# Attention and top-1 experts on one core: transposes de-interleaved on the PSUM read, masks from two iotas, unordered scatters, gathers without fills, paired score tiles

## The chip, the core and the metric

The kernel runs on one core of a Trainium2 chip. The time is the device time of one launch in microseconds (us), as the median of several runs. Beside it stands one profiled execution, from which all rows here come.

## What is computed

Attention over 4 batches of 8 heads, 768 positions of 64 numbers; heads 0, 2 and 6 see all earlier positions, the other five see four sink positions and a window of 64. Its output, seen as 3072 rows of 512, goes through an early-exit layer: a row whose skip score is positive goes to the one expert (of eight, 512 to 1024 to 512) with the highest gate logit.

```python
causal = rel >= 0                                  # rel = row - column
stream_keep = causal & (is_sink | ((rel >= 0) & (rel < window)))
mask = np.where(retr[0, :, 0, 0, None, None], causal, stream_keep)
scores = np.where(mask[None], 0.125 * (q @ k.transpose(0, 1, 3, 2)), -1e9)
a = np.exp(scores - scores.max(-1, keepdims=True))
x = (a / (a.sum(-1, keepdims=True) + 1e-09)) @ v   # to rows of 512
do_compute = x @ w_skip > 0
xc = x[do_compute]
logits = xc @ w_gate
e_idx, gate_w = argmax, and softmax at it
y[mask] = gate_w[mask, None] * (np.maximum(xc[mask] @ w1[e], 0.0) @ w2[e])   # mask = e_idx == e
out = x.copy(); out[do_compute] = xc + y
```

With the fixed draw 1163 rows are computed, by expert 69, 235, 250, 230, 53, 142, 42 and 142.

## The kernel before

The attention runs in turns `b` = 0 to 4 (the loop over `range(B + 1)` at the end of the attention part). In turn b the scores of batch b are made and, woven into them, the outputs of batch b - 1. A turn begins with `prep_v(b)` on POOL: the ones column of `va` (L249), copies of it into `vs` shifted by half a row tile (L253, L254), and zeros (L255). Then, for each of six row tiles i, comes `avx(b-1, i)` and a sixth of the steps of `front(b)`; after them `route(b-1)`, and the loads for later turns: q and k of b + 2, V of b + 2 (six DMAs, L108), and the weights of expert b + 1. All these loads convert to f16 on the way and are issued by POOL. q, k and V have two buffers each, the weights five.

`front(b)` handles four head pairs. `trans` transposes a pair's q and k on PE, six row tiles each, into a PSUM tile `tps` (64 + 64 features by six tiles by 128 rows), which is evicted to `qT` or `kT`. The rows lie in memory so that row p of tile n is position 6p + n, so the eviction writes with a stride of six elements (12 bytes); it is done in turn by DVE (L271) and ACT (L269):

```python
o = t.rearrange("c (p n) -> c n p", n=NT)
if ev[0] % 2: nc.scalar.copy(o, ps)
else:         nc.vector.tensor_copy(o, ps)
```

`retr` makes the scores of a retrieval head in three column chunks (L296, exp L301 on ACT, the triangle on DVE L307), `strm` those of a streaming head (L316 and L320, exp L323, mask `smask` on DVE L324), `sinks` those against the sink positions. `avx(b, i)` multiplies them with V (L343 to L359), normalises on DVE (L362, L363), sends the rows `x` to the output by DMA, casts them to f16 on POOL (L368, `x16`), transposes them on PE (L371, again into a `tps`), copies them to `xT` on ACT (L374) and multiplies by the gate weights (L377, `lps`, copied to `lg` on DVE, L380). The two PSUM buffers with tag "t" are shared by all transposes, gate logits and routing products; the scores have two others.

`route(b)` finds for each row its expert and its rank there (`oh`, L398; `rps`, L402 to L407), and adds its row number and gate, in three f16 parts, to the table `tab` by products with one-hot matrices (L452, L454). The table has 16 slots (two tiles of 128 for each of eight experts) by 128.

After the attention, `emp`, `idf` and `idx` (L512 to L516) turn the table into row numbers, an empty slot's being one beyond the bounds check. `gather(e)` fills `xg` with zeros on DVE (L529) and fetches its rows from the output in memory with an indirect DMA (L530), which skips empty slots. `up_(e)` casts (L550), transposes (L553), multiplies by w1 (L562) and applies ReLU; `down(e)` multiplies by w2 (L577), adds gate times result to `xg` (L579), and scatters the rows back with an indirect DMA (L581). All scatters write the same output tensor, so each waits for the one before. A branch for experts with over 256 rows (L604, L605) isn't taken here.

Which instruction stands where on its engine is set by the scheduler of the Tile framework, from the order of the code and the buffers. The DMAs of POOL's queue use eight semaphores (DMASW0 to DMASW7) in turn: one may be issued when the DMA eight before it, which had its semaphore, has landed.

Of the kernel before, what the change touches and what calls it, by code (L numbers as in the profile page):

```python
# [9 lines left out]
FP32 = mybir.dt.float32  # L10
# [41 lines left out]
def kernel(  # L52
# [59 lines left out]
    def load_w(e):  # L112
# [5 lines left out]

    load_qk(0, True)
# [12 lines left out]
    nc.vector.memset(utri, 1.0)  # L132
    nc.gpsimd.affine_select(out=utri, in_=utri, compare_op=ALU.is_ge, fill=0.0,
                            base=-1, pattern=[[1, P]], channel_multiplier=-1)
# [7 lines left out]
    nc.vector.memset(smask, 1.0)  # L142
    nc.gpsimd.affine_select(
        out=smask[:D], in_=smask[:D], compare_op=ALU.is_ge, fill=0.0,
        base=0, pattern=[[0, NT], [1, P]], channel_multiplier=-1)
    nc.gpsimd.affine_select(
        out=smask[:D], in_=smask[:D], compare_op=ALU.is_ge, fill=0.0,
        base=WINDOW - 1, pattern=[[0, NT], [-1, P]], channel_multiplier=1)

    nc.gpsimd.memset(smask[:N_SINK, 0, N_SINK:], 1.0)  # L150

    up = smask.rearrange("p i c -> p (i c)")
    nc.gpsimd.memset(up[D:, :D], 0.0)
    mid = up[D:, D:D + 5 * P].rearrange("p (i c) -> p i c", c=P)
    nc.gpsimd.affine_select(
        out=mid, in_=mid, compare_op=ALU.is_ge, fill=0.0,
        base=0, pattern=[[0, 5], [1, P]], channel_multiplier=-1)
    nc.gpsimd.affine_select(
        out=mid, in_=mid, compare_op=ALU.is_ge, fill=0.0,
        base=WINDOW - 1, pattern=[[0, 5], [-1, P]], channel_multiplier=1)  # L160
    last = up[D:, D + 5 * P:]
    nc.gpsimd.affine_select(
        out=last, in_=last, compare_op=ALU.is_ge, fill=0.0,
        base=0, pattern=[[1, D]], channel_multiplier=-1)
# [92 lines left out]
    def trans(b, pr):  # L257
        for name, src, dst in (("qT", q_in[b], qT), ("kT", k_in[b], kT)):
# [207 lines left out]
    def front(b):  # L466

        yield lambda: trans(b, 0)
        for c in range(3):
            yield lambda c=c: retr(b, 0, (0, 1), c)  # L470
            if c == 0:
                yield lambda: trans(b, 1)
# [234 lines left out]
```

## Time and profile before

| | |
|---|---|
| median of 3 runs | 318.55 us (318.13 to 319.8) |
| profiled execution | 318.38 us, span 316.6 us |
| busy PE, PE weight loads | 209.7 us, 133.7 us |
| busy DVE, ACT, POOL | 153.5, 124.7, 126.2 us |
| moved by the DMA queues | 37.7 MB, 119 GB/s on average |
| end of the last matmul | 280.15 us |

PE is TensorE, DVE is VectorE, ACT ScalarE, POOL GpSimd. A busy share over the whole span says little here, as the parts of the program have different limits; the rows below are therefore taken by stretches. In a row, "[3.86 <-DMA va]" says that the engine stood idle for 3.86 us before this instruction and that a DMA into va released it. "a<-b" names output and inputs of a group.

### The profile page before, as it was taken

To read this page: it belongs to the slowest core of one execution; us is meant where nothing else is said; L and a number is where in the kernel's file an instruction comes from. 1 tells how busy PE (TensorE), PEld (TensorE's weight loads), DVE (VectorE), ACT (ScalarE), POOL (GpSimd) and SP (SyncE) were. 2 spreads that over 40 slices of the span, in tenths; PEclk is the share of its full clock that TensorE was granted. 3 is DMA by queue.
4 is the path that set the end of the run, shared out by engine and by line. 5 is a ranking of instruction groups with operands and counts; after the bars stand their busy time and mean duration, and the time that the engine had idled before them with its cause. 6 is when DMAs were issued, how large, how long until landed. Compare 5 with 4: busy or idle time off the path is not lost. (4 is left out here: it accounts for less than half of the span.)

```text
span 316.6 us, 5049 instructions
## 1 busy us (share of the span) xinstructions
PE 209.7 (66%) x1996; PEld 133.7 (42%) x1996; DVE 153.5 (48%) x406; ACT 124.7 (39%) x137; POOL 126.2 (40%) x190
## 2 busy tenths in 40 slices
PE   0148589798755999668998897116999999930000
PEld 0133346446534546444455564104766666610000
DVE  2169354635855256896455765743444444320000
ACT  1149930869604578606676521102322222200000
POOL 8998597153328107341011112037853121222321
PEclk9999999999999999999999999999999999985555
DMA  6999999999999997911001022005499969120110
GB/s 90 158 53 143 169 206 247 224 207 223 221 183 219 236 187 103 68 35 66 35 0 68 14 88 75 28 18 153 100 188 204 219 123 167 57 81 20 41 40 6
DMA packets 53457, 37.71 MB, mean 119 GB/s; under 512 B 28706, under 2 KB 45090, under 8 KB 53424
## 3 DMA queue, kind: packets, MB, share of 16 engines
q0 software_dynamic: 49968, 31.01, 67.5%
q10 hardware_dynamic: 1728, 3.15, 2.9%
q1 hardware_dynamic: 1728, 3.15, 2.8%
q8 instruction: 17, 0.28, 0.4%
q14 instruction: 16, 0.13, 0.1%
HBM read 56.66 MB, written 10.49 MB: 212 GB/s over the span
## 5 line engine op out<-in xcount | busy, mean ns | idle before, releaser
L269 ACT COPY kT<-tps 128x768 f16<-128x768 f16 x16 | 43.5, 2716 | 26.5 <-PE tps L262 26.5
L271 DVE COPY qT<-tps 128x768 f16<-128x768 f16 x16 | 43.5, 2720 | 17.5 <-PE tps L262 17.1
L301 ACT ACTIVATE atr<-sps 128x1024 f16<-128x1024 f32 (+1 forms) x36 | 32.9, 948 | 17.7 <-PE sps L296 17.6
L581 POOL DMA_INDIRECT out_dram<-xg,idx x16 | 15.9, 997 | 56.8 <-DMA out_dram<-xg,idx 34.4
L368 POOL CAST x<-x 128x512 f16<-128x512 f32 x24 | 15.0, 627 | 43.0 <-DVE x L363 23.5
L562 PE MATMUL mhp<-mxT,w1t 128*128 128x256 f16 x256 | 30.8, 281 | 1.1 <-ACT mxT L555 0.4
L577 PE MATMUL myp<-w2t,ht 128*128 128x512 f16 x128 | 29.9, 379 | 0.0
L296 PE MATMUL sps<-qT,kT 64*128 64x512 f16 (+3 forms) x96 | 28.3, 474 | 2.0 <-ACT kT L269 2.0
L374 ACT COPY xT<-tps 128x512 f16<-128x512 f16 x24 | 14.1, 588 | 39.0 <-PE tps L371 19.4
L562 PEld LDWEIGHTS <-w1t 128*128 128x128 f16 x256 | 25.8, 101 | 7.3 <-issue 2.8
L371 PE MATMUL tps<-ident,x 128*128 128x128 f16 x96 | 15.2, 302 | 19.1 <-DVE qT L271 12.3
L352 PE MATMUL av<-va,atr 128*128 128x65 f16 x252 | 24.9, 243 | 0.0
L108 POOL DMA_DIRECT2D va<-in_v_dram x24 | 21.2, 933 | 7.5 <-DMA w1t<-in_moe_w_dram 4.9
L262 PE MATMUL tps<-ident,qin 128*64 128x128 f16 x192 | 13.7, 312 | 15.6 <-POOL ident masks.py:199 13.4
L530 POOL DMA_INDIRECT xg<-out_dram,idx x16 | 16.5, 1029 | 17.4 <-DVE idx L516 12.8
L555 ACT COPY mxT<-mtp 128x512 f16<-128x512 f16 x16 | 8.7, 588 | 35.5 <-PE mtp L553 35.5
L566 DVE TENSOR_SCALAR ht<-mhp 128x512 f16<-128x512 f32 x16 | 11.1, 692 | 23.7 <-PE mhp L562 23.7
L362 DVE RECIPROCAL rec<-av 128x4 f32<-128x4 f32 x48 | 8.5, 182 | 28.2 <-PE av L352 20.9
L343 PE MATMUL av<-vsk,esk 20*128 20x260 f16 x48 | 18.8, 394 | 2.9 <-DVE x L363 1.7
L363 DVE TENSOR_TENSOR x<-av,rec 128x256 f32<-128x256 f32 x48 | 19.9, 420 | 1.6
L352 PEld LDWEIGHTS <-atr 128*128 128x128 f16 x252 | 15.9, 123 | 9.5 <-issue 7.6
L357 PE MATMUL av<-vs,ats 128*64 128x65 f16 x120 | 19.4, 254 | 0.7 <-DVE ats L324 0.7
(131 smaller groups left out, 388.0 us busy)
## 6 DMA issues: line engine op xcount, KB each, us to landing
w1t<-in_moe_w_dram POOLq DMA_DIRECT2D x8, 1024.0 KB, 14.2
w2t<-in_moe_w_dram POOLq DMA_DIRECT2D x8, 1024.0 KB, 15.9
va<-in_v_dram POOLq DMA_DIRECT2D x24, 128.0 KB, 10.1
out_dram<-x ACTq DMA_DIRECT2D x12, 256.0 KB, 4.9
out_dram<-x SPq DMA_DIRECT2D x12, 256.0 KB, 2.8
qin<-in_q_dram POOLq DMA_DIRECT2D x3, 768.0 KB, 13.4
kin<-in_k_dram POOLq DMA_DIRECT2D x3, 768.0 KB, 17.1
qin<-in_q_dram POOLq DMA_DIRECT2D x4, 96.0 KB, 3.5
```

The lines of the kernel that those rows point to most:

```text
L108: nc.gpsimd.dma_start(out=va[b][:, i, :, :D], in_=vr[b, i])
L269: nc.scalar.copy(o, ps)
L271: nc.vector.tensor_copy(o, ps)
L296: nc.tensor.matmul(ps[i][:, o:o + w], kT[b, pr][r, j * P:(j + 1) * P], qT[b, pr][r, q0:q0 + w], start=True, stop=True)
L301: nc.scalar.activation(a[:, o:o + w], ps[i][:, :w], ACT.Exp, scale=SCALE)
L343: nc.tensor.matmul(o, esk[b % 2][:, i * P:(i + 1) * P], vsk[:, b, t], start=True, stop=False)
L352: nc.tensor.matmul(o[:, c], a[:, x0:x0 + P], va[b][:, j, h], start=False, stop=fin and j == i)
L357: nc.tensor.matmul(o[:D, c], a[:, q0:q0 + D], vs[b][:, i, u], start=False, stop=fin)
L363: nc.vector.tensor_tensor(x[:, :, t], o[:, :, :D], rec.unsqueeze(2).to_broadcast([P, 4, D]), op=ALU.mult)
L530: nc.gpsimd.indirect_dma_start(out=xg[e, t], out_offset=None, in_=out[:, :], in_offset=bass.IndirectOffsetOnAxis(ap=idx[:, sl:sl + 1], axi ...
L562: nc.tensor.matmul(hp[:, u], w1t[:, s, f * P:(f + 1) * P], xT[:, s], start=(s == 0 and u == 0), stop=(s == DS - 1 and u == 1))
L577: nc.tensor.matmul(yp, hts[e][:, f, t * P:(t + 1) * P], w2t[:, f], start=(f == 0), stop=(f == FS - 1))
```

## The change

- The eviction of the transposes reads PSUM with the stride (256 bytes from element to element) and writes contiguously.
- Two tiles of row-minus-column numbers (`rel_i`, `relh_i`) are made by three iotas on POOL ahead of the first loads. From them DVE makes ident, the triangles and the streaming mask, which were made by memsets and affine selects on POOL and DVE. An exp on one column is issued early on ACT.
- The fills of `xg` go. Gathers use the new index `idg`, in which an empty slot has the number of row 1536; scatters still use `idx`, and skip such slots.
- The scatters are declared independent of each other.
- `retr` and `strm` return their matmuls and what follows them, for one head; `both` issues the matmuls of two such tiles alternately. `front` has 13 steps in place of 15, in another order.

```diff
-    ident = const.tile([P, P], FP16, name="ident")
-    make_identity(nc, ident)
+    rel_i = const.tile([P, P], I32, name="rel_i")
+    nc.gpsimd.iota(rel_i, pattern=[[1, P]], base=0, channel_multiplier=-1)
+    relh_i = const.tile([P, P], I32, name="relh_i")
+    for x in (0, D):
+        nc.gpsimd.iota(relh_i[x:x + D], pattern=[[1, P]], base=0, channel_multiplier=-1)
     load_qk(0, True)
     load_v(0)
+    ident = const.tile([P, P], FP16, name="ident")
+    nc.vector.tensor_scalar(ident, rel_i, 0.0, None, ALU.is_equal)
-    nc.vector.memset(tri, 1.0)
-    nc.gpsimd.affine_select(out=tri, in_=tri, compare_op=ALU.is_ge, fill=0.0,
-                            base=0, pattern=[[1, P]], channel_multiplier=-1)
+    nc.vector.tensor_scalar(tri, rel_i, 0.0, None, ALU.is_ge)
...
+    band = const.tile([P, P], FP16, name="band")
+    nc.vector.tensor_scalar(band, relh_i, float(WINDOW), None, ALU.is_lt)
+    nc.vector.scalar_tensor_tensor(band, relh_i, 0.0, band, ALU.is_ge, ALU.mult)
...
+    nc.vector.tensor_copy(smask[:D], band[:D].unsqueeze(1).to_broadcast([D, NT, P]))
...
-            o = t.rearrange("c (p n) -> c n p", n=NT)
+            o = t.rearrange("c (p n) -> c p n", n=NT)
+            i_ = ps.rearrange("c n p -> c p n")
             if ev[0] % 2:
-                nc.scalar.copy(o, ps)
+                nc.scalar.copy(o, i_)
             else:
-                nc.vector.tensor_copy(o, ps)
+                nc.vector.tensor_copy(o, i_)
...
+    def both(*parts):
+        n = max(len(m) for m, _ in parts)
+        done = [0] * len(parts)
+        for i in range(n):
+            for u, (m, _) in enumerate(parts):
+                to = (i + 1) * len(m) // n if len(m) < n else i + 1
+                while done[u] < to:
+                    m[done[u]]()
+                    done[u] += 1
+        for _, post in parts:
+            post()
...
         yield lambda: trans(b, 0)
-        for c in range(3):
-            yield lambda c=c: retr(b, 0, (0, 1), c)
-            if c == 0:
-                yield lambda: trans(b, 1)
-        yield lambda: retr(b, 1, (1,), 0)
+        yield lambda: both(retr(b, 0, 0, 0), retr(b, 0, 1, 0))
+        yield lambda: trans(b, 1)
+        yield lambda: both(retr(b, 0, 0, 1), retr(b, 0, 1, 1))
+        yield lambda: both(retr(b, 0, 0, 2), retr(b, 0, 1, 2))
         yield lambda: trans(b, 2)
-        yield lambda: retr(b, 1, (1,), 1)
-        yield lambda: retr(b, 1, (1,), 2)
-        yield lambda: strm(b, 1, 0)
+        yield lambda: both(retr(b, 1, 1, 0), strm(b, 1, 0))
+        yield lambda: both(retr(b, 1, 1, 1), strm(b, 2, 0))
         yield lambda: trans(b, 3)
-        yield lambda: strm(b, 2, 0)
-        yield lambda: strm(b, 2, 1)
-        yield lambda: strm(b, 3, 0)
-        yield lambda: strm(b, 3, 1)
+        yield lambda: both(strm(b, 2, 1))
+        yield lambda: both(retr(b, 1, 1, 2), strm(b, 3, 0))
+        yield lambda: both(strm(b, 3, 1))
         yield lambda: sinks(b)
...
+        idg = rt.tile([P, NSLOT], I32, name="idg")
+        nc.vector.tensor_scalar(idg, tab[:, :, 0], float(TOK0), None, ALU.add)
...
-                nc.vector.memset(xg[e, t], 0.0)
                 nc.gpsimd.indirect_dma_start(
                     out=xg[e, t], out_offset=None, in_=out[:, :],
-                    in_offset=bass.IndirectOffsetOnAxis(ap=idx[:, sl:sl + 1], axis=0),
+                    in_offset=bass.IndirectOffsetOnAxis(ap=idg[:, sl:sl + 1], axis=0),
                     bounds_check=N - 1, oob_is_err=False)
...
-                nc.gpsimd.indirect_dma_start(
+                sc = nc.gpsimd.indirect_dma_start(
                     out=out[:, :],
                     out_offset=bass.IndirectOffsetOnAxis(ap=idx[:, sl:sl + 1], axis=0),
                     in_=xg[e, t], in_offset=None, bounds_check=N - 1, oob_is_err=False)
+                tc.declare_no_dep(sc.ins, group="sc", reason="a token has one slot")
+                tc.add_to_no_dep_group("sc", sc.ins)
```

The instructions on POOL where turn 2 begins, before: va_484 is the V buffer of batch 2, and x16_1174 and x16_1262 are the casts of the first two row tiles of batch 1.

```order
L102 DMA qin_1126<-in_q_dram 128x8x384 [waits DMASW7_49,PE_49]
L103 DMA kin_1127<-in_k_dram 128x8x384 [waits DMASW0_49,PE_49]
L249 MEMSET va_484 128x48 [waits DMASW3_49,DMASW4_49,DMASW2_49,DMASW5_49,DMASW1_49,Pool_49]
L368 CAST x16_1174<-x_1149 128x512 [waits DVE_49]
L253 COPY vs_1142<-va_484 64x6x260 [waits Pool_49]
L254 COPY vs_1142<-va_484 64x5x260 [waits Pool_49]
L253 COPY vs_1142<-va_484 64x6x65
L254 COPY vs_1142<-va_484 64x5x65
L368 CAST x16_1262<-x_1234 128x512 [waits DVE_49,PE_49,Pool_49]
```

The same place in the changed kernel, where L242 to L248 is `prep_v` and L382 the cast:

```order
L102 DMA kin_1129<-in_k_dram 128x8x384 [waits DMASW7_49,PE_49]
L242 MEMSET va_486 128x48 [waits DMASW3_49,DMASW2_49,DMASW4_49,DMASW1_49,DMASW5_49,DMASW0_49,Pool_49]
L248 MEMSET vs_1144 64x260 [waits Pool_49]
L246 COPY vs_1144<-va_486 64x6x260
L247 COPY vs_1144<-va_486 64x5x260
L246 COPY vs_1144<-va_486 64x6x65
L247 COPY vs_1144<-va_486 64x5x65
L248 MEMSET vs_1144 64x65
L382 CAST x16_1176<-x_1151 128x512 [waits DVE_49,Pool_49]
L115 DMA w2t_1777<-in_moe_w2_dram 128x8x512
L382 CAST x16_1264<-x_1236 128x512 [waits DVE_49,PE_49]
```

The cast of the first row tile stood right behind the memset that waits for V; now it stands behind the whole of `prep_v(2)`, and a weight load stands between the two casts.

POOL at the first scatters, before (xg2_1 is the second tile of expert 2):

```order
L581 DMA out_0_dram<-xg0_1_2804,idx_2794 3072x512 [waits DMASW4_49,DVE_49]
L581 DMA out_0_dram<-xg1_0_2809,idx_2794 3072x512 [waits DMASW7_49,DVE_49]
L116 DMA w2t_2889<-in_moe_w2_dram 128x8x512 [waits PE_49]
L581 DMA out_0_dram<-xg1_1_2814,idx_2794 3072x512 [waits DMASW2_49,DMASW0_49,DVE_49]
L581 DMA out_0_dram<-xg2_0_2819,idx_2794 3072x512 [waits DMASW3_49,DMASW2_49,DVE_49]
L581 DMA out_0_dram<-xg2_1_2824,idx_2794 3072x512 [waits DMASW3_49,DVE_49]
L581 DMA out_0_dram<-xg3_0_2833,idx_2794 3072x512 [waits DMASW5_49,DMASW4_49,DVE_49]
```

And in the changed kernel:

```order
L593 DMA out_0_dram<-xg0_1_2807,idx_2798 3072x512 [waits DVE_49]
L593 DMA out_0_dram<-xg1_0_2811,idx_2798 3072x512 [waits DVE_49]
L593 DMA out_0_dram<-xg1_1_2815,idx_2798 3072x512 [waits DVE_49]
L593 DMA out_0_dram<-xg2_0_2819,idx_2798 3072x512 [waits DMASW2_49,DVE_49]
L115 DMA w2t_2877<-in_moe_w2_dram 128x8x512 [waits DMASW3_49,PE_49]
L593 DMA out_0_dram<-xg2_1_2823,idx_2798 3072x512 [waits DMASW4_49,DVE_49]
L593 DMA out_0_dram<-xg3_0_2831,idx_2798 3072x512 [waits DMASW5_49,DVE_49]
```

Before, each scatter has a wait for the DMA just before it; now there is DVE's result and, from the fifth on, one semaphore each, that of the DMA eight places earlier. The second weight load of expert 7 stands behind the fifth scatter instead of the third.

DVE between the last table and the gathers, before:

```order
L454 TENSOR_TENSOR tab_199<-tbp_2742,tab_199 128x64 [waits PE_49]
L529 MEMSET xg7_0_2873 128x512
L512 TENSOR_SCALAR emp_2790<-tab_199 128x16 [waits DVE_49]
L518 SCALAR_TENSOR_TENSOR gs_2796<-tab_199 128x16
L529 MEMSET xg7_1_2878 128x512
L514 SCALAR_TENSOR_TENSOR idf_2792<-tab_199,emp_2790 128x16 [waits DVE_49]
L520 SCALAR_TENSOR_TENSOR gs_2796<-gs_2796,tab_199 128x16 [waits DVE_49]
L516 CAST idx_2794<-idf_2792 128x16 [waits DVE_49]
```

In the changed kernel, where `idg` feeds the gathers:

```order
L468 TENSOR_TENSOR tab_201<-tbp_2744,tab_201 128x64 [waits PE_49]
L522 TENSOR_SCALAR emp_2792<-tab_201 128x16 [waits DVE_49]
L527 TENSOR_SCALAR idg_2796<-tab_201 128x16
L531 SCALAR_TENSOR_TENSOR gs_2800<-tab_201 128x16
L524 SCALAR_TENSOR_TENSOR idf_2794<-tab_201,emp_2792 128x16 [waits DVE_49]
L533 SCALAR_TENSOR_TENSOR gs_2800<-gs_2800,tab_201 128x16 [waits DVE_49]
```

The fills are gone; the gathers' index comes second after the table, where `idx` came seventh.

## Rows read from the trace of the kernel before

**Rows 1.** Busy time by stretch: us, PE, PEld, DVE, ACT, POOL, clock, DMA share, GB/s.
```profile
92.00:97.00 5.00, 0.66 (x6) 0.50 (x6) 0.17 (x3) 0.00 (x0) 1.64 (x3) 1.00 1.43 223
...
200.00:211.00 11.00, 1.44 (x13) 0.92 (x13) 9.29 (x48) 0.24 (x1) 0.25 (x1) 1.00 0.00 0
...
218.00:281.00 63.00, 61.09 (x439) 41.07 (x436) 27.84 (x46) 17.16 (x30) 23.20 (x24) 1.00 0.78 151
281.00:317.00 36.00, 0.00 (x0) 0.00 (x0) 0.35 (x4) 0.00 (x0) 8.84 (x9) 0.52 0.09 30
```

**Rows 2.** Waits of the whole span, POOL: us in total, times, longest.
```profile
POOL out_dram L581 <- DMA out_dram<-xg,idx: 34.4, 9, 9.2
```

**Rows 3.** Timeline of POOL: start us, duration, operation, idle before and releaser.
```profile
210.75 1.12 POOL L530 DMA_INDIRECT xg<-out_dram,idx  x1 [12.81 <-DVE idx L516]
212.17 1.02 POOL L530 DMA_INDIRECT xg<-out_dram,idx  x1 [0.31 <-issue]
...
308.88 0.98 POOL L581 DMA_INDIRECT out_dram<-xg,idx  x1 [2.54 <-DMA out_dram<-xg,idx]
```

**Rows 4.** Timeline of DVE, routing part and end.
```profile
201.07 0.48 DVE L529 MEMSET xg<- 128x512 f32 x1
201.47 0.15 DVE L394 SCALAR_TENSOR_TENSOR w<-dl,rev 128x48 f32<-128x48 f32 x1
...
209.69 0.18 DVE L516 CAST idx<-idf 128x16 int32<-128x16 f32 x1
...
280.18 0.75 DVE L579 SCALAR_TENSOR_TENSOR xg<-myp,gs,xg 128x512 f32<-128x512 f32 x1 [0.98 <-PE cps L594]
```

**Rows 5.** Groups by line: total us, mean ns, idle before and releasers.
```profile
L271 DVE COPY qT<-tps 128x768 f16<-128x768 f16 x16 | 43.5, 2720 | 17.5 <-PE tps L262 17.1
L269 ACT COPY kT<-tps 128x768 f16<-128x768 f16 x16 | 43.5, 2716 | 26.5 <-PE tps L262 26.5
...
L316 PE MATMUL sps<-qT,kT 64*64 64x128 f16 x120 | 15.4, 308 | 3.5 <-ACT ats L323 2.5 <-ACT kT L269 0.8 <-ACT atr L301 0.2
...
L374 ACT COPY xT<-tps 128x512 f16<-128x512 f16 x24 | 14.1, 588 | 39.0 <-PE tps L371 19.4 <-DVE ol L451 10.5 <-PE tbp L452 9.0
...
L529 DVE MEMSET xg<- 128x512 f32 x16 | 7.8, 485 | 1.1 <-issue 0.3
```

**Rows 6.** Waits of PE from 138 to 196 us.
```profile
PE tps L371 <- DVE qT L271: 3.4, 3, 2.0
...
PE sps L296 <- ACT kT L269: 0.7, 1, 0.7
```

**Rows 7.** Waits of PE from 97 to 138 us.
```profile
PE tps L371 <- DVE qT L271: 3.3, 3, 2.0
PE rps L402 <- DVE oh L398: 2.0, 1, 2.0
```

**Rows 8.** Timeline of POOL, starts of turns 1, 2 and 3.
```profile
46.72 0.32 POOL L249 MEMSET va<- 128x48 f16 x1
...
51.45 1.16 POOL L368 CAST x<-x 128x512 f16<-128x512 f32 x2
...
95.30 0.32 POOL L249 MEMSET va<- 128x48 f16 x1 [3.86 <-DMA va<-in_v_dram]
95.67 0.61 POOL L368 CAST x<-x 128x512 f16<-128x512 f32 x1
...
133.03 0.32 POOL L249 MEMSET va<- 128x48 f16 x1 [2.35 <-DMA va<-in_v_dram]
...
138.22 0.61 POOL L368 CAST x<-x 128x512 f16<-128x512 f32 x1 [0.97 <-DVE hi L430]
```

**Rows 9.** Timeline of POOL, first loads.
```profile
7.21 5.36 POOL L108 DMA_DIRECT2D va<-in_v_dram  x6
...
23.23 0.91 POOL L102 DMA_DIRECT2D qin<-in_q_dram  x1
```

**Rows 10.** DMA issues at 11.4 to 12 us: KB each, us to landing.
```profile
va<-in_v_dram POOLq DMA_DIRECT2D x2, 128.0 KB, 8.8
```

More of the change, by code (lines that the diff above doesn't have):

```diff
@@ L7 @@
 from concourse._compat import with_exitstack
-from concourse.masks import make_identity
 FP32 = mybir.dt.float32
@@ L133 @@
-    nc.gpsimd.affine_select(out=utri, in_=utri, compare_op=ALU.is_ge, fill=0.0,
-                            base=-1, pattern=[[1, P]], channel_multiplier=-1)
+    nc.vector.tensor_scalar(utri, rel_i, 0.0, None, ALU.is_gt)
     ones = const.tile([P, P], FP16, name="ones")
     nc.vector.memset(ones, 1.0)
-    smask = const.tile([P, NT, P], FP16, name="smask")
[L142 to L150, printed above, removed]
-    up = smask.rearrange("p i c -> p (i c)")
[L153 to L164, printed above, removed]
+    warm = const.tile([P, 1], FP32, name="warm")
+    nc.scalar.activation(warm, ones[:, :1], ACT.Exp)
+    band = const.tile([P, P], FP16, name="band")
+    nc.vector.tensor_scalar(band, relh_i, float(WINDOW), None, ALU.is_lt)
@@ L167 @@
+    nc.vector.tensor_copy(up[D:, D + 5 * P:], band[D:, :D])
     NR = 4 * len(SINKS)
@@ L284, with retr, post @@
     CHO = ((0, 1024, 768), (1024, 1024, 640), (2048, 640, 512))
-    def retr(b, pr, heads, c):
-        ps = {}
-        for i in heads:
-            ps[i] = sp.tile([P, 1024], FP32, tag="s", name="sps")
-            if c == 0:
-                at[b, PAIRS[pr][i]] = atr.tile([P, RW], FP16, tag="atr", name="atr")
-        for j, q0, o, w in CH[c]:
-            for i in heads:
-                r = slice(i * D, (i + 1) * D)
-                nc.tensor.matmul(ps[i][:, o:o + w], kT[b, pr][r, j * P:(j + 1) * P],
-                                 qT[b, pr][r, q0:q0 + w], start=True, stop=True)
-        o, w, st = CHO[c]
-        for i in heads:
-            a = at[b, PAIRS[pr][i]]
-            nc.scalar.activation(a[:, o:o + w], ps[i][:, :w], ACT.Exp, scale=SCALE)
+    def retr(b, pr, i, c):
+        h = PAIRS[pr][i]
+        r = slice(i * D, (i + 1) * D)
+        ps = sp.tile([P, 1024], FP32, tag="s", name="sps")
+        if c == 0:
+            at[b, h] = atr.tile([P, RW], FP16, tag="atr", name="atr")
+        a = at[b, h]
+        mms = [lambda j=j, q0=q0, o=o, w=w: nc.tensor.matmul(
+            ps[:, o:o + w], kT[b, pr][r, j * P:(j + 1) * P],
+            qT[b, pr][r, q0:q0 + w], start=True, stop=True)
+            for j, q0, o, w in CH[c]]
+        def post():
+            o, w, st = CHO[c]
+            nc.scalar.activation(a[:, o:o + w], ps[:, :w], ACT.Exp, scale=SCALE)
             if c < 2:
@@ L313, in strm, with post @@
         ps = sp.tile([P, 1024], FP32, tag="s", name="sps")
+        a = ats.tile([P, S], FP16, tag="ats", name="ats")
+        at[b, PAIRS[pr][i]] = a
+        mms = []
         for n in range(NT):
             c = n * P
[L316 to L317 removed]
+            mms.append(lambda c=c: nc.tensor.matmul(
+                ps[:D, c:c + P], kt[r, c:c + D], qt[r, c:c + P], start=True, stop=True))
             lo, hi = (0 if n == 0 else c + D), min(c + D + P, S)
             for x, y in (((lo, 512), (512, hi)) if lo < 512 < hi else ((lo, hi),)):
[L320 to L325 removed]
+                mms.append(lambda c=c, x=x, y=y: nc.tensor.matmul(
+                    ps[D:, x:y], kt[r, c + D:c + P], qt[r, x:y], start=True, stop=True))
+        def post():
+            nc.scalar.activation(a, ps[:, :S], ACT.Exp, scale=SCALE)
+            nc.vector.tensor_tensor(a, a, smask.rearrange("p i c -> p (i c)"), op=ALU.mult)
+        return mms, post
+    def both(*parts):
[9 more added lines that the diff above has]
+            post()
     def sinks(b):
```

16 lines of the change are left out of this document (5 added, 11 removed).

## The prediction, made before the changed kernel was run

> **What bounds the kernel now.** I read the busy table first, then the stretches one by one, since four different limits follow each other; then, for each stretch, which wait ends last. The profiled execution took 318.38 us, 0.17 under the median of 318.55; its span is 316.6, so 1.8 us lie around the span. All sums below are made on the 318.38. About 0.5% (1.6 us) is what a measurement of this kernel can tell from no change.
>
> The stretches [rows 1]: at 92 to 97 us PE is busy for 0.66 of 5 us while the DMA share is 1.43, as high as anywhere; at 200 to 211 PE does 1.44 of 11 and DVE 9.29; at 218 to 281 PE is busy for 61.09 of 63; from 281 to 317 PE does nothing, and POOL is busy for 8.84 of 36. So an attention part that stops once for data, a routing part on DVE, an expert part on PE, and a tail that computes nothing.
>
> The tail: the wait that ends last is a scatter for the scatter before it, 34.4 us in nine waits on POOL alone [rows 2]. The sixteenth scatter issues at 308.88, although the result that it writes is ready at 280.93 [rows 3, 4]. The routing part: gathers wait for idx, written at 209.69 to 209.87; between its small operations stand memsets, and one of 0.48 us at 201.07 lets the next operation go at 201.47, 0.40 later [rows 4].
>
> The attention part: an eviction takes 2720 ns on DVE and 2716 on ACT, sixteen on each; a contiguous copy of 512 such elements from PSUM on ACT takes 588 [rows 5]. From 138 us on, in the last turns, PE's waits for them are 3.4 and 0.7 us [rows 6]. But turn 2 begins with POOL: its memset of va waits 3.86 us for the V load and runs at 95.30, the x16 cast right behind it at 95.67, and PE's transposes of x wait for that cast. Turn 3 has the same gate: memset at 133.03, cast at 138.22 [rows 8].
>
> **The change, part by part.**
>
> *Evictions.* The write becomes contiguous and the PSUM read takes on the stride. No row shows a strided PSUM read on either engine. The nearest below is the contiguous copy: 588 x 768/512 = 0.88 us; the nearest above is the old eviction with its strided write, 2.72 [rows 5]. Nothing excludes a dearer one; the rivals take that up. I take 0.9, because the same number of elements moves and the two old rows agree to 4 ns across two quite different engines, which looks like a price of the write on the SBUF side that both share. The Trainium skill, "VectorE: DVE Perf Modes", section "Mode 1× (REGULAR) — the baseline", says that this mode takes odd strides and PSUM operands alike; by it nothing is added, which no row here shows.
>
> That saves 1.8 us on each of 32, but not on the path everywhere. In turns 0 and 1 it only lets PE reach the V gate of turn 2 sooner, and that gate is set by the DMA stream. The stream starts with q(1), issued at 23.23 [rows 9]. Without the masks POOL comes to it earlier, but q(1) reuses the semaphore of the last V load of turn 0; six such loads issue from 7.21 for 5.36 us, and the last take 8.8 us to land [rows 10], so that this is not before about 11.7 + 8.8 = 20.5, with a little for the issue 21.1. So the stream, and V(2) at its end, moves by 2.1 at most: memset at 93.2 instead of 95.30. In the new order, the cast stands behind all of prep_v(2), which is what happened in turn 1 before: memset at 46.72, cast at 51.45, 4.73 us [rows 8]. So the cast goes at 97.9, 2.2 us **later** than 95.67.
>
> Inside turn 2 the faster evictions make this up (PE waits 3.3 us for qT there [rows 7]). The next gate, V(3), is released when PE's last PV products of turn 1 have read the buffer, early in turn 2's work. I put its memset within 0.5 us of 133.03 and its cast near 138.2 as before: attention up to there 0. Behind it:
> - the end of turn 2: PE's ranking matmuls waited 2.0 us for DVE's oh [rows 7], as POOL copied V beside it [rows 8]. The new order lets DVE reach it earlier; between 0 and -2.0, I take **-1.3**.
> - turn 3 and the PV of its tiles: 3.4 + 0.7 = 4.1 us of eviction waits [rows 6], each at most 2.0 long. 1.8 off the eviction leaves almost nothing: **-4.0**.
> - paired row tiles: the streaming score matmuls are 120, 15.4 us [rows 5], 3.9 a turn; most of them now alternate with another tile. At best they overlap wholly, half of 3.9, at worst nothing: **-0.7**, a third of it, as score buffers (two, now both taken by a pair) are evicted one behind the other by ACT.
>
> Attention: -6.0.
>
> *Masks from iotas.* Three iotas go ahead of the first loads on POOL and delay these by what they take, under 1 us by my estimate; DVE builds the masks where it had only memsets to do, and PE's first transposes waited for ident and not for the loads. What the masks are worth on POOL sits in the 2.1 above: the rest is hidden by the V gate, and would be worth the same few us if that didn't hold.
>
> *Fills.* Sixteen memsets of 485 ns [rows 5] go. They stand between operations that wait for each other in the routing part: ten of them delay by 0.40 each something that is waited for, -4.0; one more ahead of the last PV tile's normalisation, -0.5; and the index of the gathers now comes one operation after the table instead of three, -0.4. **-4.9.** The price: 885 of the 2048 slots are empty with this draw (my count from the reference), and now read one and the same row of 2 KB each instead of being skipped. The gather for the first tiles goes out at 210.75, 0.88 us behind idx, and the next 1.42 later [rows 3]; the issue pace stays, since the instruction walks 128 indices in either case. Bounds: 0 where the rows move inside that pace, and +2 if the first gathers land late. I take **+0.3**; the first three gathers hold mostly real rows, and the later ones have the expert stage to hide them.
>
> *Expert part.* Its operations don't change, and PE is busy for 97% of it: 0.
>
> *Unordered scatters.* Now each waits for DVE's result and for the semaphore of the DMA eight before it, which at some 7.9 us an expert (63 / 8 [rows 1]) is long done. Expert 7's last result comes at 280.93, and a scatter follows its input by about 0.88, like the gather its index: 281.8 instead of 308.88, **-27.1**. Everything that comes after the last scatter's issue (316.6 - 308.88 = 7.7 us of landing and end) comes along. Late next would be POOL's own pace (16 issues of 1 us beside weight loads): two scatters an expert leave it room. Expert 7's second weight load now stands behind five scatters instead of three, but these wait for results alone, so it goes no later.
>
> **Sum:** 318.38 - 6.0 - 4.9 + 0.3 - 27.1 = 280.7; I say **280.5 us**, the 0.17 between this execution and the median not being worth a digit.
>
> **The rivals.**
> - *The strided read costs what the strided write did.* Evictions stay at 2.7 and the late cast of turn 2 isn't made up: +2.2 instead of -6.0, so 288.7. Row for it: 2720 and 2716 could as well be a cost per element that any stride brings [rows 5]. [...] Chance 0.10.
> - *The gates don't hold.* If V(2) and V(3) come free as early as PE does, all four turns gain as the last one does: 4 x 4.1 + 2.1 in place of 4.0, with 1.3 and 0.7 as before: -20.5, so 266.2. For it: eviction waits are there in each turn. Against: POOL waited 3.86 us for V(2) with the DMA engines at their fullest [rows 1, 8]. Chance 0.12.
> - *The clock.* Cast at 97.9 with PE at the gate earlier than before makes a longer stop than the one now, some 9 us by my estimate. Before, the granted clock stayed at 1.00 (2.4 GHz) over 200 to 211, with 1.44 us of work, and fell (0.52 on average, so mostly 1.2 GHz) only in the empty tail [rows 1]. A fall here would cost the work behind it some 2 to 4 us at double durations: 284. Chance 0.08.
> - *Slower than before:* reading PSUM across is dearer still. The other terms are -4.9 + 0.3 - 27.1 = -31.7, so 32 evictions must add 31.7 + 1.6 to the path; with all of them on it, as in a chain of eviction and transposes, over 1.04 us each: 3.76 us, or 4.9 ns per element of 768 against 3.5 now. It decides from there; at 4 us an eviction 1.28 x 32 - 31.7 gives 328. No row shows either engine at such a pace. Chance 0.02.
> - *The scatters stay in a row*, through the order in which the queue lands them: 318.38 - 6.0 - 4.9 + 0.3 = 307.8. The waits are gone from the instructions, and weight loads overlapped on this queue before. Chance 0.02.
>
> **How the numbers follow.** The case of the sum has 0.62 (276 to 286, from the bounds of its terms: -2 to +2 on gathers, 0 to -2 and -1.9 on the two small ones, 0.9 to 1.4 us for the eviction), the rivals 0.10, 0.12, 0.08, 0.02 and 0.02, and 0.04 is for what I haven't thought of. From 267 to 290 the range leaves out most of the gateless case, the two last rivals and half of the unknown, under 2 in 10. Faster by over 0.5% in all but the slower rival: 0.97; same 0.01, slower 0.02.
>
> **What would show it.** In the profile of the changed kernel: the evictions at 0.8 to 1.0 us on both engines (at 2.7 the first rival); POOL's memset of va in turn 2 still waiting for the V load, near 93, and the cast after it near 98; the cast of turn 3 near 138; no memset of xg, and idx's gather within 6 us of the last gate logits; scatters in pairs at the pace of the experts, the last near 271 in its own time, and a chain that ends in one landing and not in a ladder of them. A memset in turn 2 that waits for nothing would refute the gates, and a PEclk under 9 there would point to the clock.

## The result: 282.7 us, and the profile after

The changed kernel takes 282.68 us in the median of four runs (276.55 to 283.54), against 318.69 for the kernel before in four runs. The forecast was 280.5, in a range of 267 to 290. Ratios with an interval, here 0.873 (0.862 to 0.884), count only the runs within 1.5% of a kernel's fastest, here 276.55 and a further run of 280.38, so that this one lies below the ratio of the two medians, 0.887. The profiled execution is the fastest of its runs, 276.55 us with a span of 274.6; a second profile of the same kernel, taken later, has a span of 279.9 and is nearer to the median. Both are needed to see where the time went.

Busy time by stretch, in the first profile (columns as in [rows 1]):

```profile
90.00:99.00 9.00, 0.10 (x1) 0.00 (x0) 0.42 (x1) 0.00 (x0) 4.77 (x8) 1.00 1.53 218
100.00:110.00 10.00, 10.00 (x135) 6.45 (x133) 5.34 (x16) 5.70 (x7) 3.54 (x6) 1.00 1.06 167
...
118.00:130.00 12.00, 11.63 (x124) 7.14 (x122) 7.75 (x37) 7.06 (x10) 5.52 (x11) 0.50 1.52 145
188.30:194.70 6.40, 1.44 (x13) 0.93 (x13) 5.43 (x38) 0.24 (x1) 0.00 (x0) 0.50 0.00 0
203.00:264.00 61.00, 60.22 (x436) 40.76 (x434) 26.84 (x44) 16.74 (x30) 29.96 (x31) 0.98 0.86 186
265.00:274.60 9.60, 0.00 (x0) 0.00 (x0) 0.41 (x4) 0.00 (x0) 0.98 (x1) 0.58 0.13 41
```

The stop at 90 to 99 us is longer than the one in [rows 1], the routing part is 6.4 us long instead of some 11, the expert part as full as before, and the empty end has shrunk to 9.6 us. The evictions, by line:

```profile
L265 DVE COPY qT<-tps 128x768 f16<-128x768 f16 x16 | 15.3, 958 | 14.6 <-PE tps L255 13.1 <-PE sps L288 1.4
...
L388 ACT COPY xT<-tps 128x512 f16<-128x512 f16 x24 | 14.1, 587 | 56.4 <-PE tps L385 46.0 <-DVE ol L465 10.4
...
L263 ACT COPY kT<-tps 128x768 f16<-128x768 f16 x16 | 12.8, 800 | 18.0 <-PE tps L255 18.0
```

Against [rows 5] they fell from 2720 to 958 ns on DVE and from 2716 to 800 on ACT: the read with the stride costs about what the contiguous copy does (800 against 587 x 1.5 = 881). The gates on POOL, first profile:

```profile
93.94 0.32 POOL L242 MEMSET va<- 128x48 f16 x1 [5.20 <-DMA va<-in_v_dram]
...
98.67 0.61 POOL L382 CAST x<-x 128x512 f16<-128x512 f32 x1
...
129.07 0.32 POOL L242 MEMSET va<- 128x48 f16 x1 [6.21 <-DMA va<-in_v_dram]
...
133.73 0.61 POOL L382 CAST x<-x 128x512 f16<-128x512 f32 x1
```

and second profile:

```profile
94.43 0.32 POOL L242 MEMSET va<- 128x48 f16 x1 [5.23 <-DMA va<-in_v_dram]
...
99.16 0.61 POOL L382 CAST x<-x 128x512 f16<-128x512 f32 x1
...
132.47 0.32 POOL L242 MEMSET va<- 128x48 f16 x1 [3.09 <-DMA va<-in_v_dram]
...
137.97 0.61 POOL L382 CAST x<-x 128x512 f16<-128x512 f32 x1 [0.97 <-DVE hi L444]
```

In both, the memset of turn 2 waits 5.2 us for the V load and the cast of the first row tile comes 4.73 us behind it, against 0.37 in [rows 8]. The gate of turn 3 stands where it stood in the second profile (137.97, before 138.22), and 4.5 us earlier in the first.

The route and the tail, on POOL and on DVE:

```profile
194.75 1.12 POOL L542 DMA_INDIRECT xg<-out_dram,idg  x1 [8.20 <-DVE idx L529]
...
263.54 0.98 POOL L593 DMA_INDIRECT out_dram<-xg,idx  x1 [0.74 <-DVE xg L591]
265.27 0.98 POOL L593 DMA_INDIRECT out_dram<-xg,idx  x1 [0.74 <-DVE cmx L612]
```

```profile
188.25 0.17 DVE L394 COPY lg<-lps 128x9 f32<-128x9 f32 x1 [2.20 <-PE lps L391]
...
194.10 0.17 DVE L529 CAST idx<-idf 128x16 int32<-128x16 f32 x1
...
264.24 0.75 DVE L591 SCALAR_TENSOR_TENSOR xg<-myp,gs,xg 128x512 f32<-128x512 f32 x1 [0.98 <-PE cps L608]
```

The last scatter goes out 0.28 us after its result (264.24 + 0.75 = 264.99), where it waited 28 us for its turn in [rows 3, 4]. On POOL's list of waits no scatter waits for a scatter any more; the largest in sum among those of the scatters is this one, for results:

```profile
POOL out_dram L593 <- DVE xg L591: 9.3, 5, 5.0
```

### The profile page after: what moved, and what is told of

It is laid out like the page before. It is cut to its first block, busy times and chain, and to the rows that moved or that the text cites. A ratio compares the mean times of both kernels' runs of the same rounds, so it can differ in the third digit from the quotient of the medians.

```text
span 274.6 us, 5032 instructions
## 1 busy us (share of the span) xinstructions
PE 207.7 (76%) x1996; PEld 130.6 (48%) x1996; DVE 120.9 (44%) x398; ACT 96.2 (35%) x138; POOL 121.4 (44%) x182
## 5 line engine op out<-in xcount | busy, mean ns | idle before, releaser
L382 POOL CAST x<-x 128x512 f16<-128x512 f32 x24 | 15.0, 629 | 45.4 <-DVE x L377 26.3
L388 ACT COPY xT<-tps 128x512 f16<-128x512 f16 x24 | 14.1, 587 | 56.4 <-PE tps L385 46.0
L366 PE MATMUL av<-va,atr 128*128 128x65 f16 x252 | 23.4, 236 | 7.5 <-POOL va L242 7.5
L385 PE MATMUL tps<-ident,x 128*128 128x128 f16 x96 | 14.4, 295 | 16.5 <-POOL x L382 16.5
L107 POOL DMA_DIRECT2D va<-in_v_dram x24 | 21.2, 948 | 11.4 <-DMA w2t<-in_moe_w_dram 5.3
L366 PEld LDWEIGHTS <-atr 128*128 128x128 f16 x252 | 15.0, 120 | 15.5 <-issue 13.5
L542 POOL DMA_INDIRECT xg<-out_dram,idg x16 | 16.5, 1030 | 12.8 <-DVE idx L529 8.2
L265 DVE COPY qT<-tps 128x768 f16<-128x768 f16 x16 | 15.3, 958 | 14.6 <-PE tps L255 13.1
L578 DVE TENSOR_SCALAR ht<-mhp 128x512 f16<-128x512 f32 x16 | 11.1, 691 | 23.9 <-PE mhp L574 23.9
L371 PE MATMUL av<-vs,ats 128*64 128x65 f16 x120 | 18.6, 247 | 3.7 <-POOL vs L248 2.0
L357 PE MATMUL av<-vsk,esk 20*128 20x260 f16 x48 | 18.1, 383 | 2.3 <-ACT esk L348 1.2
L263 ACT COPY kT<-tps 128x768 f16<-128x768 f16 x16 | 12.8, 800 | 18.0 <-PE tps L255 18.0
## 6 DMA issues: line engine op xcount, KB each, us to landing
w1t<-in_moe_w_dram POOLq DMA_DIRECT2D x8, 1024.0 KB, 14.1
```

The source lines that it names most:

```text
L107: nc.gpsimd.dma_start(out=va[b][:, i, :, :D], in_=vr[b, i])
L265: nc.vector.tensor_copy(o, i_)
L357: nc.tensor.matmul(o, esk[b % 2][:, i * P:(i + 1) * P], vsk[:, b, t], start=True, stop=False)
L366: nc.tensor.matmul(o[:, c], a[:, x0:x0 + P], va[b][:, j, h], start=False, stop=fin and j == i)
L371: nc.tensor.matmul(o[:D, c], a[:, q0:q0 + D], vs[b][:, i, u], start=False, stop=fin)
L542: nc.gpsimd.indirect_dma_start(out=xg[e, t], out_offset=None, in_=out[:, :], in_offset=bass.IndirectOffsetOnAxis(ap=idg[:, sl:sl + 1], axi ...
```

## The experiments

The kernels ran in three groups, each on one chip beside the kernel before, whose medians there were 318.7, 322.9 and 321.8 us. Times of whole runs are compared within a group, or as ratios to the kernel before. Stretches of the traces that end with the last gate logits are also compared across groups: the changed kernel's stand at 192.60 us in a_again and at 193.70 in a_third, further down.

### First group: repeat, scatters, evictions, place of the V preparation

**The changed kernel again** (a_again), nothing edited.

> The changed kernel once more, unaltered. Its runs so far lie between 276.6 and 283.5 us, and the profiled one is the fastest of them. In that profile PE's score products of 512 columns take 387 ns between 110 and 116 us and 605 ns in the rest of the attention part, and the profile before shows 605 ns throughout. Theory A (the spread comes from whether and where TensorE gets its faster pace in the attention part): if the profile has no such stretch, the run takes 281 to 284 us and the cast of turn 3 stands at 136 to 139 us instead of 133.7; if it has a longer one, under 276. Theory B (the spread is that of the DMA stream): the pace is the same as in the first profile, and the memset of turn 2, which waits for the V load, moves by several us between the profiles.

Measured: 281.96 us (281.11 to 284.05), cast of turn 3 at 137.97. What differs between the two profiles is TensorE's pace. PE's transposes of q and k by shape, first profile from 104 to 116 us, and then from 118 to 130:

```profile
L255 PE MATMUL tps<-ident,qin 128*64 128x128 f16 x24 | 1.1, 223 | 0.0
...
L255 PE MATMUL tps<-ident,qin 128*64 128x128 f16 x12 | 0.8, 313 | 0.0
```

Second profile, from 54 to 70 and from 100 to 130:

```profile
L255 PE MATMUL tps<-ident,qin 128*64 128x128 f16 x36 | 1.6, 223 | 0.0
...
L255 PE MATMUL tps<-ident,qin 128*64 128x128 f16 x48 | 3.4, 313 | 0.0
```

The first run had its stretch at 223 ns behind the gate of turn 2 (from 107 to 116 us) and kept the 4.5 us; the second had a longer one ahead of it (from 55 to 67), after which PE stood still for 11.9 us, waiting for a cast, instead of 4.8. So theory B falls: the memset of turn 2 differs by 0.5 us only (93.94, 94.43). Theory A doesn't hold as it was written either, for with a longer stretch the run should have taken under 276. What the two profiles fit is a theory in which the place of the stretch decides; a_third takes that up.

**Ordered scatters** (a_ordered).

```diff
-                tc.declare_no_dep(sc.ins, group="sc", reason="a token has one slot")
-                tc.add_to_no_dep_group("sc", sc.ins)
```

> The changed kernel with the scatters ordered again (the two lines that declare them independent are left out). My theory, in which the tail of the profile before was the chain of scatter and landing alone: +26 us, near 308. Rival, in which the ladder was also due to something that the other parts removed (the fills, or the late second weight load of the last expert): +10 to +20.

Measured: 308.50 us (307.41 to 313.0), +26.5 on a_again; ratio to before 0.969 (0.965 to 0.972). The ladder is back, from the last result on DVE to the last scatter on POOL:

```profile
267.73 0.75 DVE L591 SCALAR_TENSOR_TENSOR xg<-myp,gs,xg 128x512 f32<-128x512 f32 x1 [0.97 <-PE cps L606]
...
297.93 0.98 POOL L593 DMA_INDIRECT out_dram<-xg,idx  x1 [2.48 <-DMA out_dram<-xg,idx]
```

The tail was this chain and nothing else; the rival falls.

**The old eviction** (a_oldevict): output strided, PSUM read contiguous.

```diff
-            o = t.rearrange("c (p n) -> c p n", n=NT)
-            i_ = ps.rearrange("c n p -> c p n")
+            o = t.rearrange("c (p n) -> c n p", n=NT)
+            i_ = ps
```

> The changed kernel with the old eviction (contiguous PSUM read, write with the stride). Theory A of the prediction (the first two turns' gain is swallowed by the V load of turn 2): evictions back at 2.7 us, +6 to +9 us. Rival (evictions wholly on the path, 32 times 1.8 us shared by two engines): +17 to +30 us. If the memset of va in turn 2 stays at 94 us and its wait for the V load shrinks, the swallowing is shown.

Measured: 288.98 us (288.47 to 291.23), +7.0, with 2723 and 2719 ns an eviction. Sixteen on each engine became 1.8 and 1.9 us dearer, 29 us in sum on each of two engines, and a quarter of that reached the end. Where the rest goes is seen at the first PV products of turn 1, on PE, here and in the changed kernel (the profile a_third, below, in which no faster stretch mixes in):

```profile
35.17 0.27 PE L366 MATMUL av<-va,atr 128*128 128x65 f16 x2 [1.01 <-POOL va L242]
```

```profile
35.13 0.27 PE L366 MATMUL av<-va,atr 128*128 128x65 f16 x2 [7.38 <-DMA va<-in_v_dram]
```

They start at the same time. What the new evictions save in turn 0, 6.4 us, PE spends waiting for va. Late in turn 1 there is a stop that neither the prediction nor the expectation names. PE's transposes of the sixth row tile, with the old eviction and then in a_third:

```profile
80.06 0.61 PE L385 MATMUL tps<-ident,x 128*128 128x128 f16 x4 [2.36 <-POOL x L382]
```

```profile
79.61 0.60 PE L385 MATMUL tps<-ident,x 128*128 128x128 f16 x4 [4.87 <-POOL x L382]
```

The cast that they wait for stands on POOL behind the last two of the six loads of V(2), and each of these is issued only when a weight load has landed whose semaphore it uses. In a_third:

```profile
72.63 0.88 POOL L107 DMA_DIRECT2D va<-in_v_dram  x1 [5.38 <-DMA w2t<-in_moe_w_dram]
77.56 0.88 POOL L107 DMA_DIRECT2D va<-in_v_dram  x1 [4.05 <-DMA w1t<-in_moe_w_dram]
...
78.94 0.61 POOL L382 CAST x<-x 128x512 f16<-128x512 f32 x1
```

So of some 3 us that the evictions save in turn 1, 2.5 go there. At the start of turn 2 the two kernels are level: the memset waits for V here too (5.16 us, and runs at 93.88), the cast behind it goes at 98.61 (98.56 in a_third), and PE waits 9.2 us for it in both. The 7 us arise behind that: the cast of turn 3 is 4.1 us later (141.62 against 137.56), and from there to the last gate logits it takes 59.6 us instead of 56.1. Theory A holds.

**V prepared behind the fourth row tile** (a_lateprep).

```diff
-        if b < B:
-            prep_v(b)
         for i in range(NT):
...
                 f()
+            if i == 3 and b < B:
+                prep_v(b)
```

> The changed kernel with the preparation of V moved from the start of a turn to behind its fourth row tile (V of batch b is read only in turn b + 1). In the changed kernel's profile PE waits 7.5 us for va in turn 1 and 9.2 us for the cast behind the preparation in turn 2. Theory A (these gates hold back real work): -8 to -16 us, PE's waits on POOL at the start of turns 1 and 2 gone. Rival B (the DMA stream of q, k and V as such sets the pace, the gate only shows it): within 3 us, with PE waiting for q or k transposes or for later casts instead.

Measured: 277.22 us (276.54 to 277.68), -4.7; between the two. The scheduler placed the memset of turn 2 no later among POOL's work, and one cast still stands behind it and the first copy:

```profile
88.84 0.32 POOL L242 MEMSET va<- 128x48 f16 x1 [5.27 <-DMA va<-in_v_dram]
...
89.58 1.48 POOL L246 COPY vs<-va 64x1560 f16<-64x1560 f16 x1
91.01 0.61 POOL L382 CAST x<-x 128x512 f16<-128x512 f32 x1
```

It waits for V as before, 5 us earlier. So this moves the gate and doesn't lift it: neither theory is decided by it. Up to 100 us PE still waits 8.5 us for a cast and 7.8 for small copies on POOL (`skq`).

### Second group: weights later, the eviction alone, no pairing

**Expert weights later** (a_wlater).

```diff
-    load_w(0)
...
-        if b + 1 < NW and b < B:
-            load_w(b + 1)
+        for e in {1: (0, 1), 2: (2, 3), 3: (4,)}.get(b, ()):
+            load_w(e)
```

> The changed kernel with the expert weights loaded later: experts 0 and 1 behind the loads of batch 3 at the end of turn 1, 2 and 3 at the end of turn 2, 4 at the end of turn 3 (the code had one expert ahead of the first turn and one behind each of the next). Theory A (the V load of turn 2 lands late because the weights stand ahead of it in the DMA stream, and that is the gate): the memset of va in turn 2 stands under 85 us instead of 94, the time falls by 8 to 13 us, to 269 to 274. Rival B (POOL's own work, the copies of V ahead of the casts, is the gate): PE's waits for casts stay over 12 us in sum, and the time within 3 us of 282.

Measured: 270.94 us (265.58 to 272.35) against 322.89 before, a ratio of the medians of 0.839 (no interval is on record for it), where a_again has 281.96 / 318.72 = 0.885. On POOL, turn 2:

```profile
73.09 0.32 POOL L241 MEMSET va<- 128x48 f16 x1
...
79.17 0.63 POOL L381 CAST x<-x 128x512 f16<-128x512 f32 x1 [1.18 <-DVE lo L446]
```

The memset waits for nothing and stands 21 us earlier than in the changed kernel. By 0.839 x 318.7 = 267.4 the gain on a_again is some 15 us, over the 8 to 13 that theory A gave; the last gate logits come 16.8 us earlier (175.78 against 192.60). Rival B falls: PE's waits for casts are 2.9 us in sum, where a_third has 15.2. The gate was the V load behind the weights.

**Both** (a_wlater_late): the last two edits together.

> Both: weights later, and the preparation of V behind the fourth row tile. Theory A and B together: nothing of the two gates stays, 265 to 271. If the preparation of V in the middle of the turn only moves the wait to another cast: no faster than the weights alone.

Measured: 254.38 us (251.26 to 260.63), a ratio of the medians of 0.788 (no interval on record either). This is the fastest version here, and beats both kernels. Its last gate logits stand at 156.8 us. But its profile has PE at the faster pace in three stretches (53 to 58, 90 to 100 and 117 to 130 us), which a_wlater's lacks, so how much of the further 16.6 us is the edit and how much the pace isn't separated.

**The new eviction alone, in the kernel before** (b_evict): the same two lines as in the change.

> The kernel before with the new eviction alone (strided PSUM read, contiguous write). Theory A (V gates swallow what turns 0 and 1 gain): evictions at 0.8 to 1.0 us, and the time falls by 4 to 9 us, to 309 to 314, with turn 2's first cast still at 95 to 96 us. Rival (evictions on the path in each turn, since here the cast stands ahead of the copies): -15 to -25.

Measured: 312.57 us (310.0 to 313.45), ratio 0.969 (0.958 to 0.981), which is -10 us (-14 to -6); just beyond theory A's 4 to 9, and short of the rival's 15 to 25. Here the scheduler keeps the cast of turn 2 right behind the memset:

```profile
94.44 0.32 POOL L249 MEMSET va<- 128x48 f16 x1 [4.12 <-DMA va<-in_v_dram]
94.82 0.61 POOL L369 CAST x<-x 128x512 f16<-128x512 f32 x1
```

It goes at 94.82 where the changed kernel has 98.67 to 99.16. In the trace the last gate logits come 9.7 us earlier than before (189.93 against 199.64): 0.9 up to that cast, 3.0 from it to the cast of turn 3, 5.8 from there on. The eviction alone is worth about 10 us in the old order and 7 in the new one; with this interval the two can't be told apart.

**No pairing** (a_unpair): `both` runs each part's matmuls and its exp before the next.

```diff
...
+        for m, post in parts:
+            for f in m:
+                f()
+            post()
```

> The changed kernel with the two score tiles of a step made one behind the other instead of alternately (each tile's exp right behind its own matmuls), the new order of the steps kept. By the prediction's term: +0.7, at most +2, near 283. Rival (the pair holds both score buffers until both are finished, so pairing costs): -1 to -3.

Measured: 283.68 us (283.31 to 284.09), ratio 0.882 (0.873 to 0.891), which can't be told from the changed kernel's. It isn't a clean test of the pairing, as the scheduler put the cast ahead of the copies again (94.66, right behind a memset at 94.29). What can be compared is the stretch behind the gate of turn 3, cast to last gate logits: 188.05 - 132.34 = 55.7 us unpaired, 192.30 - 136.17 = 56.1 paired (a_ordered); neither has a faster stretch there. Pairing shows no gain there that is larger than 0.5 us.

### Third group: the cast, the fills, the masks

**The changed kernel a third time** (a_third).

> The changed kernel once more, beside the next three on the same chip. In the traces so far PE's transposes of q and k take 313 ns or, in stretches of some ten us that come at different places, 223. Where such a stretch lies behind the gate of turn 2, the run should take 276 to 279; where it lies ahead of it or is missing, 281 to 284.

Measured: 288.01 us (285.8 to 290.78), ratio 0.894 (0.888 to 0.900). No stretch at 223 ns anywhere, as the slower case asks; but the time lies above the 281 to 284 expected. The place of a stretch is borne out by a_fills, below: it has one from 60 to 69 us, ahead of the gate, and its cast of turn 3 comes no earlier (138.65). Up to the last gate logits a_third is like a_again (193.70 against 192.60); the rest lies in the expert part, 67.2 us from first product to last result instead of 63.2. All kernels of the second and third groups have 67 to 71 there, and those of the first 62 to 63.

**The first cast on ACT** (a_castact).

```diff
-        nc.gpsimd.tensor_copy(x16, xf)
+        if i == 0:
+            nc.scalar.copy(x16, xf)
+        else:
+            nc.gpsimd.tensor_copy(x16, xf)
```

> The changed kernel with the x16 cast of the first row tile of each turn on ACT instead of POOL; nothing else moves out of the V gate. Theory A (in turn 2 PE stands still because that cast is queued behind the memset that waits for V and behind the copies, 4.4 us of it the copies): PE's first transposes of turn 2 start at 90 to 91 us instead of 99, and the time falls by 4 to 8 us. Rival (the V load itself holds back the rest of the turn, the cast is only what is named): within 2 us, and the wait reappears at the second cast.

Measured: 274.61 us (272.83 to 278.76), -13.4 on a_third; ratio 0.850 (0.842 to 0.858). More than expected. PE's transposes of x in turn 2, and POOL's memset:

```profile
86.46 0.40 PE L388 MATMUL tps<-ident,x 128*128 128x128 f16 x2
...
94.52 0.62 PE L388 MATMUL tps<-ident,x 128*128 128x128 f16 x4
...
87.38 0.32 POOL L242 MEMSET va<- 128x48 f16 x1 [5.01 <-DMA va<-in_v_dram]
```

PE starts at 86.46, ahead of the memset, instead of at 99. But the memset also came 6.4 us earlier (87.38 against 93.82), because the scheduler now put one weight load behind the V load that had stood ahead of it. Seven such loads stand ahead in a_third, six here, two in a_wlater, and the memset stands at 93.8, 87.4 and 73.1. So the 13.4 us hold both: the cast out of the queue, and one megabyte less in front of V. The rival falls all the same, as the wait doesn't reappear at the second cast (PE's waits for casts are 1.5 us in sum).

**Fills back** (a_fills): memset of xg, and gathers by idx.

```diff
+                nc.vector.memset(xg[e, t], 0.0)
...
-                    in_offset=bass.IndirectOffsetOnAxis(ap=idg[:, sl:sl + 1], axis=0),
+                    in_offset=bass.IndirectOffsetOnAxis(ap=idx[:, sl:sl + 1], axis=0),
```

> The changed kernel with the fills of xg and the gathers by idx put back (empty slots are skipped again). By the prediction's terms: +4.9 for the memsets and the later index, -0.3 for the 885 rows, so +4.6; by the two profiles, in which the last gate logits stand 11.1 us ahead of the first gather before and 6.5 after, and the first expert product 7.2 and 7.9 us behind it: +3.9. Rival (the memsets fill gaps): 0 to +1.5.

Measured: 294.49 us (290.05 to 296.55), +6.5 in the medians, but the two ranges touch; by the ratios, 0.907 (0.898 to 0.916) against 0.894, it is +4.2. The trace agrees with that: from the last gate logits to the first expert product there are 213.73 - 195.51 = 18.2 us, and 207.79 - 193.70 = 14.1 in a_third: +4.1. The first gather goes out 11.1 us behind the logits, 6.5 in a_third:

```profile
206.58 1.12 POOL L543 DMA_INDIRECT xg<-out_dram,idx  x1 [12.77 <-DVE gs L533]
...
195.51 0.17 DVE L394 COPY lg<-lps 128x9 f32<-128x9 f32 x1 [0.85 <-PE lps L391]
...
196.34 0.48 DVE L542 MEMSET xg<- 128x512 f32 x1
...
205.60 0.10 DVE L529 CAST idx<-idf 128x16 int32<-128x16 f32 x1
```

**Old masks** (a_masks): the part with memsets and affine selects put back, no iotas, no early exp.

> The changed kernel with the masks of the kernel before (memsets and affine selects on POOL, no iotas ahead of the first loads, no early exp). Theory A (the start is hidden by the V gate): q(1) issues about a microsecond later, the memset of va in turn 2 moves by as much, from 94 to 95, and the time by +0.5 to +2. Rival (PE's start at 13 instead of 7 us is on the path): +4 to +6.

Measured: 290.46 us (289.66 to 291.27), +2.5; ratio 0.902 (0.896 to 0.909). PE's first transposes again wait 13.4 us for ident, and the gate moves by 1.3:

```profile
23.23 0.91 POOL L102 DMA_DIRECT2D qin<-in_q_dram  x1
...
95.14 0.32 POOL L250 MEMSET va<- 128x48 f16 x1 [5.21 <-DMA va<-in_v_dram]
...
99.87 0.61 POOL L390 CAST x<-x 128x512 f16<-128x512 f32 x1
...
138.86 0.61 POOL L390 CAST x<-x 128x512 f16<-128x512 f32 x1 [0.97 <-DVE hi L452]
```

In a_third these stand at 21.94, 93.82, 98.56 and 137.56. PE's late start (13.4 us, where a_third's first transposes go at 4.4 and the rest from 5.9 on) costs 1.3 at the gate and 1.6 at the last gate logits (195.27 against 193.70): hidden, as theory A says; the median lies half a microsecond above its range, within the spread of the runs.

## Why the prediction was right, point by point

The time between the same events, in us; a plus is later or longer than before:

| from, to | before | predicted | first profile | second profile |
|---|---|---|---|---|
| start, cast of turn 3 | 138.22 | 0 | -4.5 | -0.3 |
| cast of turn 3, last gate logits | 61.42 | -6.0 | -6.9 | -6.8 |
| last logits, first gather | 11.11 | -4.9 | -4.6 | -4.6 |
| first gather, first expert product | 7.16 | +0.3 | +0.8 | +0.8 |
| first product, last result | 63.02 | 0 | -0.7 | +0.2 |
| last result, end of the span | 35.67 | -27.1 | -26.1 | -26.0 |
| sum | | -37.7 | -42.0 | -36.7 |

- *Evictions.* 0.9 us forecast, 0.96 and 0.80 measured. The first rival falls, at 288.7 (its terms add up to 288.9). The Trainium skill, "PSUM — Partial Sum Buffer", section "Specifications (TRN2)", says that a non-contiguous pattern there slows matmuls; no run here tries that. These reads by DVE and ACT show no such price: at a step of 256 bytes they cost some 0.83 ns per further element on ACT, an estimate from two rows ((800 - 588) / 256). The Trainium skill, "VectorE: DVE Perf Modes", section "Mode 1× (REGULAR) — the baseline", says that odd strides and PSUM operands all work in that mode. A read with both took 958 ns here, which agrees; no contiguous copy on DVE stands beside it.
- *The V gate of turn 2.* Memset forecast at 93.2, measured 93.8 to 94.4; cast at 97.9, measured 98.6 to 99.2. a_wlater and the three counts of weight loads show that it is the load behind the weights, a_oldevict that stops on POOL swallow nearly all that the evictions save in turns 0 and 1. V(1) does so already in turn 1, and so does the cast of the sixth row tile, behind V(2)'s issues; the prediction had looked at neither. The rival without gates falls.
- *Turn 3.* Forecast: unchanged. So it is where TensorE keeps one pace up to there or is fast too early (137.6 to 138.0), and as the balance that the prediction made it: the cast of turn 2 comes 2.9 to 3.5 us later than before, and the evictions give 4.0 back behind it (39.0 us from cast to cast in a_third, 43.0 in a_oldevict). The first profile's -4.5 goes with a stretch of the faster pace behind turn 2's gate, which the prediction did not think of.
- *Behind the gate of turn 3.* -6.0 as a sum nearly held (-5.3 in a_third, -6.8 and -6.9 in the table), but by luck in its parts. The -1.3 for PE's ranking matmuls of turn 2 did not come, for in a_third they wait 2.2 us for DVE's oh where they waited 2.0; they also stand ahead of the cast of turn 3, in the stretch that was forecast at 0. The -0.7 for **paired row tiles** isn't seen in the trace. The -4.0 of the evictions is 3.5 by a_oldevict and 5.8 by b_evict. By a_oldevict some 1.8 us come from something else that changed, such as the order of the steps; it was not separated.
- *Fills.* -4.9 and +0.3; measured -4.6 and +0.8, and +4.1 for both in a_fills. From first gather to first product a_fills, which skips the empty slots again, takes 7.15 us, a_third 7.61 and the two profiles of the table 7.9: so reading them costs 0.5 to 0.8 us, not 0.3. Whether it is that all read the same row was not tried.
- *Scatters.* -27.1, and a_ordered gives 26.5. Two sizes inside were off and nearly cancel: the last scatter follows its result by 0.28 us and not 0.88, but what comes behind it takes 9.3 us and not 7.7, which a_ordered also has (305.68 - 297.93 = 7.75), as unordered scatters land later (below). Nor was the DMA eight places earlier always "long done": in the first profile a scatter at 241.58 waits 3.06 us for a weight load, and the first one goes 11.8 us behind its result. From 252.41 on they follow their results by 0.28, so it cost nothing at the end.
- *Masks.* "Hidden by the V gate", 2.1 at most; measured 1.3 at the gate in a_masks.
- *The clock rival.* At the stop of turn 2 the granted clock stays at 1.00 in the first profile and in a_third. It falls elsewhere: in the first profile to 0.50 (1.2 GHz) before 118 us, behind the faster stretch, and PE's transposes then took 313 ns, no longer than at the 1.00 of before. Against that pace it cost nothing in the attention part. The rival was wrong in its premise that 1.00 granted means the faster pace.

## What to carry to other kernels

When a trace shows a stop that a DMA ends, count what stands ahead of that DMA in its queue before speeding up the work in front of it: here 29 us less of evictions on each of two engines gave 7, while moving weight loads that nothing needed for another 100 us gave some 15. A small operation queued behind one that waits inherits the whole wait; where the order comes from a scheduler, look at where it put it after each edit, as an edit elsewhere (the pairing, the cast) moved it here. And a chain of transfers that are ordered only because they write one tensor is worth its full length when nothing else follows.

## What the runs showed that was not expected

**TensorE's pace is not its granted clock.** In the whole attention part of the kernel before, at a granted 1.00, transposes took 313 ns and 512-column scores 605. In the first profile of the changed kernel transposes took 223 ns and such scores 387 from 107 to 116 us, with PE busy for 10.00 of 10 us from 100 to 110; then the granted clock fell to 0.50, where it is from 118 on, and they took 313 and 605 again. Of twelve profiles of the changed kernel and its variants five have such stretches, at different places: the first, a_again, a_unpair, a_wlater_late and a_fills. In these five, and in no other, the granted clock falls within the attention part, each time behind such a stretch. What brings one on stays open: in a_third PE is as busy, 10.00 of each ten us from 100 to 130, and keeps 313.

**Unordered scatters land later.** The median from issue to landing, of before and then of the changed kernel:

```profile
out_dram<-xg,idx POOLq DMA_INDIRECT x16, 2.7
```

```profile
out_dram<-xg,idx POOLq DMA_INDIRECT x16, 7.4
```

**The start of the expert part can take 4 to 8 us more.** In the second and third groups of runs PE is not full there in the first 16 us; in a_masks the granted clock is 0.79 in the second eight of them, in a_third it is 1.00 throughout, and the products come late all the same. It is not explained, and it is why whole runs of different groups are not compared in microseconds.
